# Sparse attention and a squared-ReLU layer on one core: squaring in place, eight mask products on GpSimd, new priorities

## The chip, the cores and the metric

The kernel runs on one core of a Trainium2 chip. The core has a matrix engine (TensorE, PE in the profile), VectorE (DVE), ScalarE (ACT), GpSimd (POOL) and SyncE (SP), and 16 DMA engines that all queues share. POOL and SP issue all the DMAs here. The metric is device time in microseconds of a whole execution; lower is better.

## The reference

Eight batches of eight heads, 576 positions, head size 64. Heads 0 to 3 see a band of 32 positions, heads 4 to 7 every 32nd position. The result, as 4608 tokens of 512, goes through a layer with a squared ReLU.

```python
mask_local = (rel >= 0) & (rel < 32)                    # heads 0..3
mask_strided = (rel >= 0) & (pos[None] % 32 == pos[:, None] % 32)   # heads 4..7
scores = np.where(mask, q @ k.T / 8, -1e9)
attn = softmax(scores)
x = (attn @ v).transpose(0, 2, 1, 3).reshape(4608, 512)
h = x @ w_in                                            # 512 -> 2048
r = np.maximum(h, 0.0)
out = (s * (r * r) + b) @ w_out                         # 2048 -> 512
```

## The kernel before

**Attention.** Each batch is four pairs of heads: m = 0 and 1 are band pairs ("loc"), 2 and 3 strided pairs ("str"). For a pair PE makes the scores of only those blocks that the mask can reach (`score`, L656, into a bank `ps_s`), ACT takes their exponential into `p_loc` or `p_str` (L674), and from batch 1 on one product per pair with a 0/1 mask clears what the mask forbids (`ms`, L682, on DVE, in place). Then PE multiplies by V (`av`, L717, into the banks `ps_a` and `ps_t`), whose rows carry a column of ones, so that the sums of the softmax come with them; DVE inverts those (L734) and scales (L744) into `x_nat`. There are two `p_loc` and two `p_str` tiles, and one bank each of `ps_a` and `ps_t` in the late batches, so that each group of six value products waits for the scaling of an earlier one. `x_nat` is transposed into `xT`, on PE or, later, by DMAs of the SP queue.

**The layer.** Tokens go in nine blocks T of 512. `ff1` (L1016) makes h for 128 features at a time, `rl` (L1042, L1044) the ReLU into a tile `u` of a pool `up` with three buffers of two features each, `sq` (L1050, L1052) the square of such a pair into `gT`, which has two buffers of 16 features. `ff2` (L1271) multiplies by `w_out`. From T = 2 on, `ff2_seven` (L984) does with seven products of half size what takes eight: DVE forms sums of pieces of `gT` (L852) and adds up the products (L903, L915, L926). For T = 7 and 8 `ff1_seven` (L1241) does the same in the first matmul, with ReLU by `add` (L1161) and `relu` (L1169, L1172) into `u` and the square at L1182 and L1184.

**What sets the order.** No engine chooses at run time: each works through its own queue in the order of the program, and PE is where the streams meet. That order comes from a planner (`Plan`) which runs while the program is written. Each PE step, and each piece of work of the other engines ("post"), has keys that it needs, a cost in ns for each engine that may do it, and keys that it makes. Each time that PE's clock moves, the posts that are ready go to the engine that would end first, by their ready time plus a priority from a table `ORDER`; there are four tables, for four stretches of the planner's clock (`UNTIL`). The planner has one clock for each engine and knows of nothing that one engine does to another's speed. POOL's posts are the loads of the next batches (`fetch_qk`: L1356, L387, L390, L405; `fetch_v`: L415, L420), which need the POOL queue for about 0.75 us each, and a few copies.

Of the kernel before, what the change touches and what calls it, by code (L numbers as in the profile page):

```python
# [10 lines left out]
FP16 = mybir.dt.float16  # L11
# [128 lines left out]
class Step:  # L140
    def __init__(self, fn, ns, needs=(), group=None, keys=(), posts=(), after=None):
# [80 lines left out]
def lay_out(ctx, tc, nc, q, k, v, moe_w_in, moe_w_out, moe_s, moe_b, out, order, q_shape, out_shape,  # L222
# [41 lines left out]
    up = ctx.enter_context(tc.tile_pool(name="up", bufs=3))  # L264
# [216 lines left out]
    PE_MASK = 1  # L481
    ps = {f"{tag}{i}": psum.tile([128, PS], FP32, name=f"ps_{tag}{i}")
# [24 lines left out]
    def pair_steps(b, m):  # L507
# [135 lines left out]
        def score(i, group):  # L643
# [18 lines left out]
            if i % per_s == n - 1:  # L662
                key = ("s", id_, g)
                s.keys = [key]

                ng = nt // per_s + (nt % per_s > 0)

                def ex(eng):
                    if "whole" not in st:
                        st["whole"] = p_bufs[loc][p_taken[loc] % len(p_bufs[loc])]  # L670
                        p_taken[loc] += 1
                    at = g * 2 * per_s * nq
                    st["pw", g] = st["whole"][:, at:]
                    nc.scalar.activation(  # L674
                        out=st["pw", g][0:nk, 0:2 * n * nq],
                        in_=st["s", g][0:nk, 0:2 * n * nq], func=AF.Exp, scale=scale)

                def ms(eng):
                    pt = st["whole"][:, 0:2 * nt * nq].rearrange("k (t c) -> k t c", c=nq)
                    mask = (mask_loc if loc else mask_str)[:, None, :].to_broadcast(  # L680
                        [nk, 2 * nt, nq])
                    nc.vector.tensor_tensor(out=pt[0:nk], in0=pt[0:nk], in1=mask, op=ALU.mult)  # L682

                free = [("a", (b - 1, m), 1 if loc else 2)] if b else []
                s.posts = [([key] + free, {"A": 170 + 0.83 * 2 * n * nq}, ex,
                            [("p" if b < PE_MASK else "e", id_, g), group])]
                if b >= PE_MASK and g == ng - 1:
                    s.posts.append(([("e", id_, x) for x in range(ng)],
                                    {"V": 150 + 0.52 * 2 * nt * nq}, ms,
                                    [("p", id_, x) for x in range(ng)]))  # L690
# [315 lines left out]
    def ff1(T, ft, ct, group, cts=(0, 1, 2, 3), early=False):  # L1006
# [23 lines left out]
        if ct == cts[-1]:  # L1030
# [6 lines left out]
            def rl(eng):  # L1037
                if at % 2 == 0:
                    gts["u", T, pair] = up.tile([128, 2, PS], FP16, tag="u", name="u")
                u = gts["u", T, pair][:, at % 2]  # L1040
                if eng == "A":
                    nc.scalar.activation(out=u, in_=gts["h", T, ft], func=AF.Relu)  # L1042
                else:
                    nc.vector.tensor_relu(out=u, in_=gts["h", T, ft])  # L1044

            def sq(eng):
                u = gts["u", T, pair]
                g = gts[T][:, pair[0]:pair[0] + 2, :]
                if eng == "A":
                    nc.scalar.activation(out=g, in_=u, func=AF.Square)  # L1050
                else:
                    nc.vector.tensor_tensor(out=g, in0=u, in1=u, op=ALU.mult)  # L1052

            first = at // 2 * 2
            free = ([("g", T, ff_order(T)[first - 6])] if first >= 6 else
                    [("g", T - 1, ff_order(T - 1)[first - 6])] if T else [])
            s.posts = [([key] + free, {"A": 600, **({"V": 690} if T == 0 else {})}, rl, [("u", T, ft), group])]
# [62 lines left out]
    def ff1_seven():  # L1120
# [3 lines left out]
        for at, (T, u) in enumerate(units):  # L1124
# [28 lines left out]
            def u_at(row, j, st=st, ft=ft):  # L1153
                if ("u", row) not in st:
                    st["u", row] = (xnp if row else up).tile(
                        [128, 2, PS], FP16, tag="xs" if row else "u", name="u")
                return st["u", row][:, :, 256 * j:256 * j + 256]
# [17 lines left out]
            def square(row, st=st, T=T, ft=ft):  # L1175
                def g(eng):
                    if T not in gts:
                        gts[T] = gp.tile([128, NFT, PS], FP16, tag="gT", name="gT")
                    x = st["u", row]
                    g_ = gts[T][:, ft + 8 * row:ft + 8 * row + 2, :]  # L1180
                    if eng == "A":
                        nc.scalar.activation(out=g_, in_=x, func=AF.Square)  # L1182
                    else:
                        nc.vector.tensor_tensor(out=g_, in0=x, in1=x, op=ALU.mult)  # L1184
# [5 lines left out]
            def was(x, old=old):  # L1190
                return [(x,) + old] if old else []

            far = ff_order(T - 1)[8 + 4 * u:12 + 4 * u] if u < 2 else [
                x + y for x in (ft - 4, ft + 4) for y in (0, 1)]
            free = [("g", T - 1 if u < 2 else T, x) for x in far]
# [12 lines left out]
            def wn(n, ft=ft):  # L1208
# [18 lines left out]
                        ([key("c21"), key("c22"), ("F2", T - 2)], SQR, square(1),  # L1227
# [3 lines left out]
                        ([key("c11"), key("c12"), ("F2", T - 2)], SQR, square(0),  # L1231
# [406 lines left out]
```

## Time and profile before

| | us |
|---|---|
| runs of the kernel | 297.75 median (297.03 to 298.77, 3 runs) |
| profiled execution: span from first to last instruction | 295.5 |
| what lies around the span: median less span | 2.25 |
| PE busy | 289.5 (98%) |
| DVE busy | 236.8 (80%) |
| ACT busy | 194.6 (66%) |
| POOL busy | 92.8 (31%) |

Of the profiled execution the page gives the span alone; the 2.25 us beside it are what the runs have more. Only an engine that sets the end can shorten the time when it gets less to do; work of another engine counts where PE has to wait for it.

### The profile page before, as it was taken

The numbers are of one execution on the slowest core, as the hardware profiler recorded it, in microseconds if no ns is written. First come the engines' busy times: TensorE is split into PE (matmuls) and PEld (weight loads), VectorE is DVE, ScalarE is ACT, GpSimd is POOL, SyncE is SP. The second block draws the span as 40 slices with busy tenths as digits, with TensorE's granted clock in tenths as the row PEclk, the third lists the DMA queues.
The fourth block names the chain that finished last, engine by engine and source line by source line (L and its number), as shares of the span: only waits on it lengthen the run. The fifth ranks groups of instructions, "written<-read, shape, count | busy, mean of one in ns | idle before, by whom it ended". The sixth has DMA issues, their size and how long they took to land.

```text
span 295.5 us, 7106 instructions
## 1 busy us (share of the span) xinstructions
PE 289.5 (98%) x2803; PEld 219.3 (74%) x2803; DVE 236.8 (80%) x498; ACT 194.6 (66%) x334; POOL 92.8 (31%) x140
## 2 busy tenths in 40 slices
PE   7899999999999999999999999999999999999995
PEld 3775655665565567989867785779888999999984
DVE  5765977888976789768986888688899689888874
ACT  3667855897967797947873777478966564576500
POOL 8872623610961396008820195200002000000000
PEclk9999999999999999999999999999999999999999
DMA  8999999999999699979999999998430300210314
GB/s 131 180 206 203 213 184 174 208 189 128 140 160 145 98 91 161 160 138 146 162 149 147 169 168 130 134 137 213 44 104 13 109 35 2 71 38 0 109 39 143
DMA packets 106152, 38.19 MB, mean 129 GB/s; under 512 B 85414, under 2 KB 103974, under 8 KB 106118
## 3 DMA queue, kind: packets, MB, share of 16 engines
q0 software_dynamic: 60848, 18.23, 64.2%
q1 hardware_dynamic: 45270, 19.51, 36.1%
q8 instruction: 22, 0.36, 0.5%
q14 instruction: 12, 0.10, 0.1%
HBM read 36.99 MB, written 10.62 MB: 161 GB/s over the span
## 4 chain that ended last, share of the span: by engine, by line
PE 95%; POOL 3%; DVE 1%; issue 1%; ACT 0%; POOLq 0%
PE ps_f L1016 32%; PE ps_f L984 25%; PE ps_f L1271 8%; PE ps_s L656 5%; PE ps_f L1241 3%; PE ps_a L717 3%; PE ps_t L1241 2%; PE ps_s L984 2%; PE ps_a L1241 2%; PE ps_s L1241 2%; PE ps_t L717 1%; PE ps_t L984 1%; PE ps_s L1271 1%; PE ps_f L717 1%; PE ps_t L535 1%; PE ps_f L535 1%
## 5 line engine op out<-in xcount | busy, mean ns | idle before, releaser
L1016 PE MATMUL ps_f<-xT,w_in_sb 128*128 128x512 f16 (+4 forms) x568 | 115.3, 331 | 0.0
L1042 ACT ACTIVATE u<-ps_f 128x512 f16<-128x512 f32 x107 | 62.8, 595 | 34.5 <-PE ps_f L1016 32.4
L1016 PEld LDWEIGHTS <-w_in_sb 128*128 128x128 f16 x576 | 57.1, 114 | 23.1
L984 PEld LDWEIGHTS <-gT 128*128 128x128 f16 x608 | 58.3, 98 | 8.6
L984 PE MATMUL ps_f<-w_out_sb,gT 128*128 128x256 f16 x376 | 53.4, 273 | 0.0
L1271 PE MATMUL ps_f<-w_out_sb,gT 128*128 128x512 f16 x112 | 31.9, 379 | 0.0
L674 ACT ACTIVATE p_str<-ps_s 72x432 f16<-72x432 f32 (+1 forms) x45 | 21.1, 488 | 10.1 <-PE ps_s L656 9.5
L1052 DVE TENSOR_TENSOR gT<-u 128x1024 f16<-128x1024 f16 x32 | 21.8, 682 | 5.2 <-ACT u L1042 4.8
L1050 ACT ACTIVATE gT<-u 128x1024 f16<-128x1024 f16 x24 | 25.4, 1058 | 0.7
L984 PE MATMUL ps_f<-w_mix,gT 128*128 128x256 f16 x176 | 24.9, 273 | 0.0
L674 ACT ACTIVATE p_loc<-ps_s 128x384 f16<-128x384 f32 x46 | 20.7, 489 | 5.5 <-PE ps_s L656 5.1
L744 DVE TENSOR_TENSOR x_nat<-ps_a,rec 72x384 f16<-72x384 f32 (+2 forms) x45 | 23.5, 523 | 0.7
L852 DVE TENSOR_TENSOR gT<-gT 128x1024 f16<-128x1024 f16 x34 | 22.4, 683 | 0.3 <-ACT gT L1050 0.3
L415 POOL DMA_DIRECT2D v_loc<-in_v_dram x24 | 17.8, 767 | 10.1 <-DMA w_out_sb<-in_moe_w_out_dram 4.2
L984 PEld LDWEIGHTS <-S 128*128 128x128 f16 x176 | 17.1, 98 | 2.7
L717 PEld LDWEIGHTS <-p_str 72*128 72x128 f16 x256 | 13.6, 98 | 5.8 <-ACT p_str L674 0.7
L420 POOL DMA_DIRECT2D v_str<-in_v_dram x16 | 13.0, 817 | 12.8 <-PE ps_f L1016 3.7
L1271 PEld LDWEIGHTS <-gT 128*128 128x128 f16 x128 | 11.4, 98 | 6.9 <-issue 0.2
L1356 POOL COPY gate<-kT 1x1 f16<-1x1 f16 x6 | 2.2, 371 | 45.0 <-DMA kT<-ks 45.0
L984 PE MATMUL ps_f<-w_mix,S 128*128 128x256 f16 x112 | 15.0, 273 | 0.0
L734 DVE RECIPROCAL rec<-ps_a 72x6 f32<-72x6 f32 (+2 forms) x45 | 8.3, 184 | 8.4 <-PE ps_a L717 8.0
L717 PEld LDWEIGHTS <-p_loc 128*128 128x128 f16 x192 | 11.2, 98 | 5.0 <-ACT kTs L437 0.8
(235 smaller groups left out, 543.1 us busy)
## 6 DMA issues: line engine op xcount, KB each, us to landing
out_dram<-o SPq DMA_DIRECT2D x34, 256.0 KB
w_in_sb<-in_moe_w_in_dram POOLq DMA_DIRECT2D x4, 512.0 KB, 9.9
w_out_sb<-in_moe_w_out_dram POOLq DMA_DIRECT2D x4, 512.0 KB, 10.7
qs<-in_q_dram POOLq DMA_DIRECT2D x6, 288.0 KB, 8.1
ks<-in_k_dram POOLq DMA_DIRECT2D x6, 288.0 KB, 9.9
v_loc<-in_v_dram POOLq DMA_DIRECT2D x24, 72.0 KB, 9.8
ql<-in_q_dram POOLq DMA_DIRECT2D x4, 288.0 KB, 9.9
kl<-in_k_dram POOLq DMA_DIRECT2D x16, 72.0 KB, 3.7
```

The source lines that it names most:

```text
L415: nc.gpsimd.dma_start(out=vl[LPAD:128, h, :, 0:D], in_=v_band(b, h))
L674: nc.scalar.activation(out=st["pw", g][0:nk, 0:2 * n * nq], in_=st["s", g][0:nk, 0:2 * n * nq], func=AF.Exp, scale=scale)
L717: nc.tensor.matmul(out=st["pa", g][:, n % 6, :], lhsT=st["pw", gp_][0:nk, i * nq:i * nq + WIDE], rhs=vt[0:nk, 2 * mm + e, j, :])
L744: nc.vector.tensor_tensor(out=x_at(0, cnt), in0=st["pa", g][0:nq, 0:cnt, 0:D], in1=st["rec", g][0:nq, 0:cnt].to_broadcast([nq, cnt, D]), o ...
L852: {"V": nc.vector, "P": nc.gpsimd}[eng].tensor_tensor(out=at(out), in0=at(x), in1=at(y), op=op)
L984: nc.tensor.matmul(out=gts[name, T, t][:, 0] if halves else gts[name, T][:, t], lhsT=lhs(k, t), rhs=rhs(k), start=fresh and k == 0 and (ha ...
L1016: nc.tensor.matmul(out=gts["h", T, ft][:, lo:hi], lhsT=w_in_sb[ft // 4][:, ct].rearrange("p (x l) -> p l x", l=4)[:, ft % 4], rhs=xT[ct][: ...
L1042: nc.scalar.activation(out=u, in_=gts["h", T, ft], func=AF.Relu)
L1050: nc.scalar.activation(out=g, in_=u, func=AF.Square)
L1052: nc.vector.tensor_tensor(out=g, in0=u, in1=u, op=ALU.mult)
L1241: nc.tensor.matmul(out=st[bk][:, 256 * t:256 * t + 256], lhsT=lhs(t, c), rhs=rhs(c), start=fresh and t == c == 0, stop=t == c == 1, skip_g ...
L1271: nc.tensor.matmul(out=gts[id_], lhsT=gts[T][:, ft, ts * 128:(ts + 1) * 128], rhs=w_out_sb[:, ft, cols], start=(ft == 0), stop=(ft == NFT ...
```

## The change

Three things.

1. `u` and its pool go. ReLU writes straight into its place in `gT`, and the square is taken there in place, on ACT or DVE as before, with as many instructions of the same sizes. With `u` gone, the ReLU has no wait for a free buffer of it; for T = 7 and 8 the adds and ReLUs now wait until `ff2` of block T - 2 has read its `gT` (key `("F2", T - 2)`), where only the squares did.
2. The mask products of the two band pairs of batches 4 to 7, eight of them, go from DVE to GpSimd (`POOL_MASK = 4`). The planner has them at 4000 ns.
3. All four priority tables have other numbers.

```diff
 UNTIL = (26000.0, 110000.0, 215000.0)
 ORDER = [
-    {"g": 0.0, "S": -2500.0, "in": 500.0, "w_mix": 2500.0, "wc": 0.0, "ev": 2500.0, "c21": -200.0,
...
+    {"g": 0.0, "S": -400.0, "in": -1500.0, "w_mix": 1000.0, "wc": -400.0, "ev": 2500.0,
...
-    up = ctx.enter_context(tc.tile_pool(name="up", bufs=3))
...
+    POOL_MASK = 4
...
-                    nc.vector.tensor_tensor(out=pt[0:nk], in0=pt[0:nk], in1=mask, op=ALU.mult)
+                    on(eng)(out=pt[0:nk], in0=pt[0:nk], in1=mask, op=ALU.mult)
...
                     s.posts.append(([("e", id_, x) for x in range(ng)],
+                                    {"P": 4000.0} if b >= POOL_MASK and loc else
                                     {"V": 150 + 0.52 * 2 * nt * nq}, ms,
...
-                if at % 2 == 0:
-                    gts["u", T, pair] = up.tile([128, 2, PS], FP16, tag="u", name="u")
-                u = gts["u", T, pair][:, at % 2]
+                u = gts[T][:, ft]
...
-                    nc.scalar.activation(out=g, in_=u, func=AF.Square)
+                    nc.scalar.activation(out=g, in_=g, func=AF.Square)
                 else:
-                    nc.vector.tensor_tensor(out=g, in0=u, in1=u, op=ALU.mult)
+                    nc.vector.tensor_tensor(out=g, in0=g, in1=g, op=ALU.mult)
...
-            s.posts = [([key] + free, {"A": 600, **({"V": 690} if T == 0 else {})}, rl, [("u", T, ft), group])]
+            s.posts = [([key], {"A": 600, **({"V": 690} if T == 0 else {})}, rl, [("u", T, ft), group])]
...
-            far = ff_order(T - 1)[8 + 4 * u:12 + 4 * u] if u < 2 else [
-                x + y for x in (ft - 4, ft + 4) for y in (0, 1)]
-            free = [("g", T - 1 if u < 2 else T, x) for x in far]
+            free = [("F2", T - 2)]
```

PE's queue holds the same 2801 matmuls before and after. The first 456 and the last 252 of them stand in the same order; between, the value products of the band pairs of batches 4 to 7 move back. Ahead of the first one of batch 6 (pair 0) there stand, beside what stood there, 8 matmuls of `ff1` of 512 columns, 42 of `ff2_seven` of 256, 16 scores of 144 and 12 value products of 65.

On POOL's queue, before, these are the loads of batch 7: two small copies that wait for the transposed k of batch 6 (`gate`), then q and k, then V.

```order
L1356 COPY gate<-kT_2571 1x1 x2
L387 DMA ql<-in_q_dram 96x6x64 x4
L387 DMA kl<-in_k_dram 96x6x64 x4
L405 DMA qs<-in_q_dram 72x4x512
L405 DMA ks_120<-in_k_dram 72x4x512
L415 DMA v_loc_102<-in_v_dram 96x6x64 x4
L420 DMA v_str_104<-in_v_dram 72x8x64 x4
```

The same place on POOL's queue after the change, and the queue's end:

```order
L1346 COPY gate<-kT_2536 1x1 x2
L387 DMA ql<-in_q_dram 96x6x64 x4
L387 DMA kl<-in_k_dram 96x6x64 x4
L405 DMA qs<-in_q_dram 72x4x512
L405 DMA ks_117<-in_k_dram 72x4x512
L683 TENSOR_TENSOR p_loc_112<-p_loc_112,masks 128x1152
L683 TENSOR_TENSOR p_loc_113<-p_loc_113,masks 128x1152
L415 DMA v_loc_99<-in_v_dram 96x6x64 x4
L420 DMA v_str_101<-in_v_dram 72x8x64 x4
L683 TENSOR_TENSOR p_loc_112<-p_loc_112,masks 128x1152
L683 TENSOR_TENSOR p_loc_113<-p_loc_113,masks 128x1152
```

The two mask products of batch 6 stand behind the gate and the ten loads of q and k of batch 7, and ahead of that batch's V; the last two are those of batch 7. Batch 5 stands in the same way, both products between k and V of the next batch.

POOL's queue after the change at batch 4, where it has its first mask product:

```order
L405 DMA ks_117<-in_k_dram 72x4x512
L683 ISA
L683 TENSOR_TENSOR p_loc_112<-p_loc_112,masks 128x1152
L415 DMA v_loc_99<-in_v_dram 96x6x64 x4
L420 DMA v_str_101<-in_v_dram 72x8x64 x4
L683 TENSOR_TENSOR p_loc_113<-p_loc_113,masks 128x1152
```

The second product has eight loads of V ahead of it, and the first one an instruction without a tile (`ISA`) that before stood ahead of POOL's only product of two tensors, `Ub`, behind all loads.

On DVE's queue, before, at batch 5 (`p_loc_115` and `p_loc_116` are its band pairs, `p_str_117` its first strided pair, `o` stores of block T = 2):

```order
L915 SCALAR_TENSOR_TENSOR o<-ps_f_163,sb_all,Vb 128x512
L682 TENSOR_TENSOR p_loc_115<-p_loc_115,masks 128x1152
L915 SCALAR_TENSOR_TENSOR o<-ps_f_162,sb_all,Ua 128x512
L437 COPY qD_str_110<-qT_2094 64x8x72 x2
L734 RECIPROCAL rec<-ps_a_159 96x6
L734 RECIPROCAL rec<-ps_t_156 96x6
L682 TENSOR_TENSOR p_loc_116<-p_loc_116,masks 128x1152
L744 TENSOR_TENSOR x_nat<-ps_a_159,rec 96x6x64
L744 TENSOR_TENSOR x_nat<-ps_t_156,rec 96x6x64
L915 SCALAR_TENSOR_TENSOR o<-ps_f_163,sb_all,Ub 128x512
L734 RECIPROCAL rec<-ps_a_159 96x6
L682 TENSOR_TENSOR p_str_117<-p_str_117,masks 72x1152
```

The same place on DVE's queue after the change (`p_str_114` is the first strided pair of batch 5):

```order
L917 SCALAR_TENSOR_TENSOR o<-ps_f_160,sb_all,Vb 128x512
L437 COPY qD_str_106<-qT_2060 64x8x72 x2
L917 SCALAR_TENSOR_TENSOR o<-ps_f_159,sb_all,Ua 128x512
L437 COPY qD_str_107<-qT_2060 64x8x72 x2
L917 SCALAR_TENSOR_TENSOR o<-ps_f_160,sb_all,Ub 128x512
L905 SCALAR_TENSOR_TENSOR Va<-ps_f_159,sb_all,bcs 128x512
L854 TENSOR_TENSOR gT<-gT 128x4x256
L683 TENSOR_TENSOR p_str_114<-p_str_114,masks 72x1152
L854 TENSOR_TENSOR gT<-gT 128x4x256
L736 RECIPROCAL rec<-ps_a_156 72x6
L683 TENSOR_TENSOR p_str_115<-p_str_115,masks 72x1152
```

The band pairs' products are gone from it, their scaling (`x_nat` 96x6x64) stands further back, and a sum of two pieces of `gT` now stands right ahead of the first strided pair's product, for which PE's next value products wait.

More of the change, by code (lines that the diff above doesn't have):

```diff
@@ L1046, in sq @@
             def sq(eng):
-                u = gts["u", T, pair]
                 g = gts[T][:, pair[0]:pair[0] + 2, :]
                 if eng == "A":
-                    nc.scalar.activation(out=g, in_=u, func=AF.Square)
+                    nc.scalar.activation(out=g, in_=g, func=AF.Square)
                 else:
[L1052 to L1056, printed above, removed]
-            s.posts = [([key] + free, {"A": 600, **({"V": 690} if T == 0 else {})}, rl, [("u", T, ft), group])]
+                    nc.vector.tensor_tensor(out=g, in0=g, in1=g, op=ALU.mult)
+            s.posts = [([key], {"A": 600, **({"V": 690} if T == 0 else {})}, rl, [("u", T, ft), group])]
             if at % 2:
@@ L1151, in keep, with u_at @@
                 return g
[L1153 to L1157, printed above, removed]
+            def u_at(row, j, T=T, ft=ft):
+                if T not in gts:
+                    gts[T] = gp.tile([128, NFT, PS], FP16, tag="gT", name="gT")
+                return gts[T][:, ft + 8 * row:ft + 8 * row + 2, 256 * j:256 * j + 256]
             def add(row, j, of, name, st=st, u_at=u_at):
@@ L1173, in relu, with square @@
                         "p (t x) -> p t x", t=2))
-            def square(row, st=st, T=T, ft=ft):
+            def square(row, T=T, ft=ft):
                 def g(eng):
-                    if T not in gts:
-                        gts[T] = gp.tile([128, NFT, PS], FP16, tag="gT", name="gT")
-                    x = st["u", row]
                     g_ = gts[T][:, ft + 8 * row:ft + 8 * row + 2, :]
                     if eng == "A":
-                        nc.scalar.activation(out=g_, in_=x, func=AF.Square)
+                        nc.scalar.activation(out=g_, in_=g_, func=AF.Square)
                     else:
-                        nc.vector.tensor_tensor(out=g_, in0=x, in1=x, op=ALU.mult)
+                        nc.vector.tensor_tensor(out=g_, in0=g_, in1=g_, op=ALU.mult)
                 return g
@@ L1226, in ff1_seven @@
                          [key("c21"), Dd]),
-                        ([key("c21"), key("c22"), ("F2", T - 2)], SQR, square(1),
+                        ([key("c21"), key("c22")], SQR, square(1),
                          [("g", T, ft + 8), ("g", T, ft + 9)])]),
@@ L1230, in ff1_seven @@
                        [([key("p3")] + free, COPY, relu, [key("c12"), A]),
-                        ([key("c11"), key("c12"), ("F2", T - 2)], SQR, square(0),
+                        ([key("c11"), key("c12")], SQR, square(0),
                          [("g", T, ft), ("g", T, ft + 1)])]),
```

77 rows, old and new, of the table ORDER are left out of this document.

## The prediction

> **What bounds the kernel now.** I read the page first, then PE's waits, a table by stage, and the last microseconds.
>
> ```profile
> span 295.5 us, 7106 instructions
> PE 289.5 (98%) x2803; PEld 219.3 (74%) x2803; DVE 236.8 (80%) x498; ACT 194.6 (66%) x334; POOL 92.8 (31%) x140
> PE   7899999999999999999999999999999999999995
> ```
>
> PE is busy in every one of the 40 slices but the first two and the last. PE's own waits, and two stretches of the middle (us, then busy time of PE, PEld, DVE, ACT and POOL, clock, DMA share, GB/s):
>
> ```profile
> PE ps_t L527 <- DMA ql<-in_q_dram: 0.9, 1, 0.9
> PE ps_s L1521 <- PEq L1622: 0.8, 1, 0.8
> PE ps_f L717 <- DVE v_loc L437: 0.7, 1, 0.7
> PE ps_f L717 <- POOL v_loc L437: 0.4, 1, 0.4
> ...
> 110.00:160.00 50.00, 50.00 (x495) 40.24 (x494) 40.38 (x86) 35.00 (x59) 19.73 (x30) 1.00 1.36 151
> 160.00:215.00 55.00, 55.00 (x526) 42.66 (x524) 44.91 (x97) 39.45 (x68) 14.22 (x20) 1.00 1.25 143
> ```
>
> All of PE's waits together are 2.8 us, and each of the four belongs to the first batch. From 110 to 215 us, where the change does its work, PE is busy for 105 of 105 us at full clock, while DVE is at 81% of it. So no work taken from DVE, ACT or POOL there can shorten the kernel. What can lengthen it is a result that comes later than PE gets to it. The first 456 matmuls keep their order, so the waits of the start stay; the last 252 keep theirs too, and behind the last matmul stands this tail of 3.1 us:
>
> ```profile
> 291.32 1.04 PE L984 MATMUL ps_f<-w_out_sb,S 128*128 128x256 f16 x8
> ...
> 292.40 0.48 DVE L915 SCALAR_TENSOR_TENSOR o<-ps_f,sb_all,Ub 128x256 f32<-128x256 f32 x1 [0.39 <-PE ps_f L984]
> ```
>
> A gain has no place to come from. The question is what new waits PE gets.
>
> **The change, part by part.** First the squares in place and the products that leave DVE:
>
> ```profile
> L1052 DVE TENSOR_TENSOR gT<-u 128x1024 f16<-128x1024 f16 x32 | 21.8, 682 | 5.2 <-ACT u L1042 4.8
> L852 DVE TENSOR_TENSOR gT<-gT 128x1024 f16<-128x1024 f16 x34 | 22.4, 683 | 0.3 <-ACT gT L1050 0.3
> L682 DVE TENSOR_TENSOR p_loc<-p_loc,masks x14: 714/752/759, 37.0 to 204.3; 128x1152 f16<-128x1152 f16 x14
> ```
>
> DVE takes 683 ns to write over its own input (L852) and 682 from `u` to `gT`, so its squares cost what they did. On ACT no row shows a square in place; I take no change, and ACT's idle third covers some tens of ns more or less. The ReLUs lose a wait that PE never felt, and the adds of T = 7 and 8 gain one whose PE order is unchanged; I put both at 0. Eight products leave DVE: 8 x 0.752 = 6.0 us of its time, worth 0 on PE's path.
>
> What such a product costs on POOL no row shows. The nearest is POOL's only product of two tensors, L926, a quarter of whose time lies beside DVE work (timeline of both engines; start and duration in us):
>
> ```profile
> L926 POOL TENSOR_TENSOR Ub<-Ua,bcs x1: 1649/1649/1649, 221.5 to 221.5; 128x512 f32<-128x512 f32 x1
> L852 DVE TENSOR_TENSOR S<-gT x18: 677/683/1140, 94.3 to 282.6; 128x1024 f16<-128x1024 f16 x18
> ...
> 221.38 0.67 DVE L1099 TENSOR_TENSOR ks<-ks,w_in_sb 128x1024 f16<-128x1024 f16 x1
> 221.54 1.65 POOL L926 TENSOR_TENSOR Ub<-Ua,bcs 128x512 f32<-128x512 f32 x1 [33.35 <-DVE Ua L903]
> 222.60 1.14 DVE L852 TENSOR_TENSOR S<-gT 128x1024 f16<-128x1024 f16 x1 [0.55 <-PE ps_f L984]
> ```
>
> Two things stand here. The DVE sum that starts at 222.60, inside the POOL product (221.54 to 223.19), takes 1.14 us where the median is 0.683: it looks held until POOL is done. And POOL, which starts while DVE is in L1099 (to 222.05), may itself have been held until then, so that 512 elements took 223.19 - 222.05 = 1.14 us. By that rate 1152 elements take 2.6 us, by the whole 1649 ns 3.7 us. I take 2.9: the lower rate and 0.3 for a DVE operation that is under way when POOL comes (half of 0.68). [...]
>
> [...] None of DVE's stores or scalings, which read one tensor from PSUM, ran beside L926; I take them to go on. Now each batch. PE positions come from the row of before, plus or minus the matmuls that the new order puts ahead, at these prices: 0.109 us for 256 columns (16 in 1.75), 0.216 for 512 (8 in 1.73), 0.063 for a score of 144 (3 in 0.19), 0.032 for a value product (6 in 0.19).
>
> ```profile
> 94.06 1.73 PE ps_f L1016 x8
> 263.54 1.75 PE ps_s L984 x16
> 59.80 0.35 PE L656 MATMUL ps_s<-qD_str,kTs 128*72 128x144 f16 x3
> 59.99 0.38 PE L1016 MATMUL ps_f<-xT,w_in_sb 128*128 128x512 f16 x1
> 170.88 0.35 PE L717 MATMUL ps_a<-v_loc,p_loc 128*128 128x65 f16 x6
> 171.07 0.32 PE L717 MATMUL ps_t<-v_loc,p_loc 128*128 128x65 f16 x5
> ```
>
> Batch 6. Its first value products stood at 170.88; 8 x 0.216 + 42 x 0.109 + 16 x 0.063 + 12 x 0.032 = 7.7 us more stand ahead: PE comes at 178.6. The product for them stands in POOL's queue behind the k load of batch 7, which ends at 176.8:
>
> ```profile
> 176.09 0.77 POOL L405 DMA_DIRECT2D ks<-in_k_dram  x1
> ...
> 141.46 0.79 POOL L405 DMA_DIRECT2D ks<-in_k_dram  x1
> 146.97 0.35 PE L717 MATMUL ps_a<-v_str,p_str 72*128 72x65 f16 x6
> 145.07 0.71 DVE L682 TENSOR_TENSOR p_str<-p_str,masks 72x1152 f16<-72x1152 f16 x1
> ```
>
> 176.8 + 2.9 = 179.7: PE waits 1.1 us. The second product ends 2.9 later, 3.5 us of matmuls further on: in time. V of batch 7 is issued some 6 us later than now, ten or more ahead of its use: 0.
>
> Batch 5. The k load ends at 142.2, so POOL is in its two products from 142.2 to 148.0. In DVE's queue a sum of `gT` and the first strided mask product stand there; both wait until 148.0, then take 0.68 + 0.71: 149.4. PE's value products for them stood at 146.97 and now have 10 x 0.109 more and 0.216 + 24 x 0.032 less ahead, so 147.1: PE waits 2.3 us.
>
> Batch 7. POOL has no load left ahead; DVE's product on the first pair began at 200.91 and the scores stand 0.3 us later, so POOL works from 201.2 to 207.0. Two sums and the strided product wait in DVE: 207.0 + 2 x 0.68 + 0.71 = 209.1. PE's value products stood at 209.97 and 2.8 us less stand ahead (ten pairs of 128 and 384 columns, each pair at the price of 512, two of 256, twelve value products): 207.2. PE waits 1.9 us.
>
> ```profile
> 200.91 0.76 DVE L682 TENSOR_TENSOR p_loc<-p_loc,masks 128x1152 f16<-128x1152 f16 x1 [0.22 <-ACT p_loc L674]
> 209.97 0.35 PE L717 MATMUL ps_a<-v_str,p_str 72*128 72x65 f16 x6
> ...
> 108.70 0.75 POOL L405 DMA_DIRECT2D ks<-in_k_dram  x1
> 109.41 3.03 POOL L415 DMA_DIRECT2D v_loc<-in_v_dram  x4
> 112.43 2.43 POOL L420 DMA_DIRECT2D v_str<-in_v_dram  x3
> 113.12 1.21 DVE L878 TENSOR_TENSOR w_out_sb<-w_out_sb 128x2048 f16<-128x2048 f16 x1
> 115.65 0.41 DVE L882 TENSOR_TENSOR bcs<-bcs 128x256 f32<-128x256 f32 x1
> ...
> 113.28 0.35 PE L717 MATMUL ps_a<-v_loc,p_loc 128*128 128x65 f16 x6
> 118.11 0.35 PE L717 MATMUL ps_a<-v_str,p_str 72*128 72x65 f16 x6
> ```
>
> Batch 4. POOL's first product runs from 109.4 to 112.3 and holds back a square, the sum of `bcs`, a `w_mix` difference and the strided product in DVE, 3.0 us together (0.69, 0.4, 1.2, 0.71): 115.3. PE stood there at 118.11 and has 2.6 us less ahead (nine pairs of 192 and 320 columns, two scores and 24 value products less, two of 256 more): 115.5. In time, barely. But SP's queue has one store more ahead of the transposes that open POOL's gate, and its product ends later; if the gate opens 2 us later, PE waits 1.8. I take the middle, 0.9. The second product stands behind eight loads of V (3.03 + 2.43 + 0.8 = 6.3 us): 112.3 + 6.3 + 2.9 = 121.5, and PE comes at 113.28 + 10.1 = 123.4 (32 such pairs, 8 scores, 15 of 256, 32 value products). In time by 1.9.
>
> The sum: 0.9 + 2.3 + 1.1 + 1.9 = 6.2 us. The profiled span would go from 295.5 to 301.7; the median of the runs, 2.25 us above the span, from 297.75 to 304.0. With 2.6 us for a product and the gate as now the four are 0, 1.7, 0.8 and 1.3: 301.6. With 3.7 and the gate 2 us later they are 2.6, 3.9, 1.9 and 3.5: 309.7.
>
> **The rivals.** First, DVE is not held: the 1.14 us was something else. Only one row of eighteen shows it, and L1099, under way when POOL began, took its usual 0.67. Against it: that one row is the only sum beside a POOL product. Then only batch 6's queue costs, 1.1 us: 298.9.
>
> Second, all is hidden, and the time is not above the present one. It turns on POOL's rate: in batch 6 there are 178.6 - 176.8 = 1.8 us, in batch 5 (147.1 - 1.4 - 142.2) / 2 = 1.75, in batch 7 1.95. A product of under 1.75 us costs nothing anywhere. POOL's copies run at such a rate:
>
> ```profile
> L437 POOL COPY v_str<-vs 72x512 f16<-72x512 f16 x4 | 2.3, 611 | 2.1 <-DMA vs<-in_v_dram 2.1
> L926 POOLq MODIFY_POOL_CONFIG  x2: 42/42/42, 188.2 to 188.2; - x2
> ```
>
> 611 ns for 512 is 1.4 us for 1152, but with one input; the row with two needs 2.6. The same end comes if PE reaches these places later than I place it, or the gates open earlier. The time would be 297.8, and since only the start could give anything back, hardly less.
>
> Third, POOL stands still at the instruction ahead of its first product. Before, it was done at 188.2 and the product came 33 us later, so a pause there could not be seen; now nothing lies between. Batch 4 then pays: its second product has 1.9 us of room, and each us beyond that is one of PE. With a pause of 5 us that is 3.1 us in place of 0.9: 306.2. [...]
>
> **How the numbers follow.** Forecast 304.0 with chance 0.58, its own range 301.6 to 309.7. Not held: 0.15, 298.9. All hidden: 0.13, 297.8. The pause: 0.11, 306 to 308. What is left, 0.03, is a gain, which no row offers. Half a per cent, 1.5 us, is about what a measurement of this kernel can tell from no change, so slower means above 299.2: 0.58 + 0.11 and 0.04 of the case not held, 0.73; the same is 0.13 and the other 0.11 of it, 0.24; faster 0.03. From 298.0 to 309.8 about 8 in 10 lie.
>
> **What would show it.** PE waits on POOL `p_loc` in batch 6 and on DVE `p_str` in batches 5 and 7, 1 to 2.5 us each, and PE's slices below 9 there. POOL's rows of L683 between 2.6 and 3.7 us. DVE rows of L854, L1051 and L683 of 2 us and more beside them, and nowhere else. If DVE's rows stay at 0.7 us beside POOL's products, the main term is wrong; if POOL's rows are under 1.8 us, all of it is; if a gap stands between the k load and POOL's first product, it is the third rival.

## The result, and the profile after

The changed kernel takes 320.71 us (median of 4 runs, 316.07 to 323.36), the kernel before 297.61 beside it; the ratio is 1.068 (95% interval 1.061 to 1.074). The forecast was 304.0 with 298.0 to 309.8: the sign was right, the size far too small. Ratios here leave out executions that count as slow (over 1.5% above the fastest of the same kernel), 321.81 and 323.36 among these four, so they are not the quotients of the medians. The profiled execution is the longest of the four, 323.36 us with a span of 321.6. The spans of the others are 314.3, 317.8 and 320.0; the mean granted clock goes from 0.984 in the two shortest to 0.973 in the longest, which is a part of the scatter and not all of it.

The page of the kernel after (span; PE's busy tenths and granted clock in 40 slices):

```profile
span 321.6 us, 7087 instructions
...
PE   8899999999999977997799938999699999999995
...
PEclk9999999999999989999799995999799999999999
```

PE has holes now, four groups of them, and in one slice of each group the clock is low as well. PE's waits (us in total, how many, the longest) and the stretches of the prediction, with one more (us, then busy time of PE, PEld, DVE, ACT, POOL; granted clock, DMA share, GB/s; in the last stretch PE was busy for 35.00 us at clock 1.00 before):

```profile
PE ps_a L719 <- DVE p_str L683: 8.2, 2, 6.0
PE ps_s L657 <- DVE qD_str L437: 6.2, 2, 3.6
PE ps_t L719 <- DMA v_str<-in_v_dram: 1.7, 1, 1.7
...
110.00:160.00 50.00, 42.53 (x397) 34.55 (x395) 43.38 (x66) 28.14 (x50) 31.75 (x38) 0.93 1.51 131
160.00:215.00 55.00, 48.57 (x392) 33.27 (x391) 41.02 (x75) 30.34 (x50) 19.37 (x23) 0.94 1.09 128
215.00:250.00 35.00, 31.76 (x324) 26.74 (x322) 31.03 (x62) 23.26 (x37) 7.11 (x3) 0.95 0.33 74
```

The first three waits are five places, one or two in each of batches 4 to 7: 16.1 us. The clock of 0.93, 0.94 and 0.95 costs, by an estimate, 0.07 x 50 + 0.06 x 55 + 0.05 x 35 = 8.5 us more. Together 24.6 of the 26.1 us by which this span grew. In the shortest execution the clock of 0.984 leaves 0.016 x 314.3 = 5.0 us for that term.

What DVE and GpSimd did there (timeline, start and duration in us; L683 is the mask product, L1051 a square, L854 a sum of `gT`, L437 a copy of Q into `qD_str`, x2 two rows in one):

```profile
111.58 4.11 DVE L1051 TENSOR_TENSOR gT<-gT 128x1024 f16<-128x1024 f16 x1
111.93 0.72 POOL L405 DMA_DIRECT2D ks<-in_k_dram  x1
112.75 2.39 POOL L683 TENSOR_TENSOR p_loc<-p_loc,masks 128x1152 f16<-128x1152 f16 x1
...
123.61 2.37 POOL L683 TENSOR_TENSOR p_loc<-p_loc,masks 128x1152 f16<-128x1152 f16 x1
123.68 2.87 DVE L1051 TENSOR_TENSOR gT<-gT 128x1024 f16<-128x1024 f16 x1
126.47 0.54 DVE L746 TENSOR_TENSOR x_nat<-ps_t,rec 96x384 f16<-96x384 f32 x1
127.06 0.34 PE L719 MATMUL ps_t<-v_str,p_str 72*128 72x65 f16 x6 [1.66 <-DMA v_str<-in_v_dram]
...
147.71 6.84 DVE L437 COPY qD_str<-qT 64x576 f16<-64x576 f16 x1
149.65 4.72 POOL L683 TENSOR_TENSOR p_loc<-p_loc,masks 128x1152 f16<-128x1152 f16 x2
...
186.07 7.09 DVE L854 TENSOR_TENSOR gT<-gT 128x1024 f16<-128x1024 f16 x1
187.88 4.71 POOL L683 TENSOR_TENSOR p_loc<-p_loc,masks 128x1152 f16<-128x1152 f16 x2
...
222.06 4.87 POOL L683 TENSOR_TENSOR p_loc<-p_loc,masks 128x1152 f16<-128x1152 f16 x2 [23.36 <-ACT p_loc L675]
222.24 4.86 DVE L437 COPY qD_str<-qT 64x576 f16<-64x576 f16 x2
```

Read the ends first. The held copy ends at 147.71 + 6.84 = 154.55, 0.2 us after GpSimd's second product (154.37); the held sum at 193.16, 0.6 after (192.59); the square at 115.69, 0.6 after (115.14). So each DVE row lasts until GpSimd is done, and then takes its own 0.2 to 0.6 us. Now the starts. In batches 5 and 6 one DVE row spans both products, and in batches 4 to 6 it begins 1.2 to 1.9 us before the product's row, while GpSimd still shows loads. In batch 7, with no loads right ahead, two copies share 4.86 us: DVE came in between the two products there. The wait at 127.06 is put down to a load of V, but those value products need bank `ps_t`, whose scaling (L746) stood behind the square held until 126.55 and ended at 127.01.

What is open: whether the products alone do this or the new order, what the low clock comes from, and why the hold begins early.

### The profile page after: what moved, and what is told of

It reads as the page before. It is cut to its first block, busy times and chain, and to the rows that moved or that the text cites. A ratio compares the mean times of both kernels' runs of the same rounds, so it can differ in the third digit from the quotient of the medians.

```text
span 321.6 us, 7087 instructions
## 1 busy us (share of the span) xinstructions
PE 298.6 (93%) x2803; PEld 223.0 (69%) x2803; DVE 255.6 (79%) x496; ACT 191.4 (60%) x330; POOL 112.0 (35%) x146
## 4 chain that ended last, share of the span: by engine, by line
PE 78%; DVE 8%; POOL 6%; DMA 4%; issue 3%; SPq 1%; POOLq 0%
PE ps_f L1018 26%; PE ps_f L986 20%; PE ps_f L1261 7%; PE ps_s L657 3%; DVE qD_str L437 3%; DMA v_str<-in_v_dram 3%; PE ps_f L1231 3%; DVE gT L854 3%; PE ps_a L719 2%; PE ps_t L1231 2%; PE ps_s L1231 2%; PE ps_s L986 2%; PE ps_a L1231 2%; PE ps_t L719 1%; PE ps_t L986 1%
## 5 line engine op out<-in xcount | busy, mean ns | idle before, releaser
L1018 PE MATMUL ps_f<-xT,w_in_sb 128*128 128x512 f16 (+4 forms) x568 | 121.6, 341 | 0.0
L1042 ACT ACTIVATE gT<-ps_f 128x512 f16<-128x512 f32 x107 | 63.1, 595 | 44.2 <-PE ps_f L1018 43.4
L986 PE MATMUL ps_f<-w_out_sb,gT 128*128 128x256 f16 x376 | 54.9, 276 | 1.1 <-DVE Va L905 1.1
L1051 DVE TENSOR_TENSOR gT<-gT 128x1024 f16<-128x1024 f16 x32 | 27.5, 860 | 7.6 <-ACT gT L1042 7.1
L1261 PE MATMUL ps_f<-w_out_sb,gT 128*128 128x512 f16 x112 | 29.7, 379 | 0.0
L854 DVE TENSOR_TENSOR gT<-gT 128x1024 f16<-128x1024 f16 x34 | 28.8, 869 | 0.3 <-ACT gT L1049 0.3
L683 POOL TENSOR_TENSOR p_loc<-p_loc,masks 128x1152 f16<-128x1152 f16 x8 | 19.1, 2409 | 23.5 <-ACT p_loc L675 23.4
L1049 ACT ACTIVATE gT<-gT 128x1024 f16<-128x1024 f16 x24 | 25.4, 1057 | 0.7
L746 DVE TENSOR_TENSOR x_nat<-ps_a,rec 96x384 f16<-96x384 f32 (+2 forms) x46 | 24.1, 525 | 0.9
L736 DVE RECIPROCAL rec<-ps_a 96x6 f32<-96x6 f32 (+2 forms) x46 | 8.5, 185 | 15.6 <-PE ps_a L719 15.4
L719 PE MATMUL ps_a<-v_str,p_str 72*128 72x65 f16 x146 | 9.6, 198 | 8.2 <-DVE p_str L683 8.2
```

What stands on the lines that cost most here:

```text
L683: on(eng)(out=pt[0:nk], in0=pt[0:nk], in1=mask, op=ALU.mult)
L719: nc.tensor.matmul(out=st["pa", g][:, n % 6, :], lhsT=st["pw", gp_][0:nk, i * nq:i * nq + WIDE], rhs=vt[0:nk, 2 * mm + e, j, :])
L746: nc.vector.tensor_tensor(out=x_at(0, cnt), in0=st["pa", g][0:nq, 0:cnt, 0:D], in1=st["rec", g][0:nq, 0:cnt].to_broadcast([nq, cnt, D]), o ...
L854: {"V": nc.vector, "P": nc.gpsimd}[eng].tensor_tensor(out=at(out), in0=at(x), in1=at(y), op=op)
L986: nc.tensor.matmul(out=gts[name, T, t][:, 0] if halves else gts[name, T][:, t], lhsT=lhs(k, t), rhs=rhs(k), start=fresh and k == 0 and (ha ...
L1018: nc.tensor.matmul(out=gts["h", T, ft][:, lo:hi], lhsT=w_in_sb[ft // 4][:, ct].rearrange("p (x l) -> p l x", l=4)[:, ft % 4], rhs=xT[ct][: ...
```

## The experiments

### Which of the three parts costs

**All products on DVE, planned anew for that** (new tables, squares in place):

```diff
-    POOL_MASK = 4
+    POOL_MASK = 8
```

> Kernel after, with the batch from which GpSimd takes the mask products set to 8, so that DVE does all of them and the order is worked out anew for that; new priority tables and squares in place stay. My theory (GpSimd's products hold DVE, PE starves, its clock drops): no DVE row of L683, L854 or L1051 above 1.3 us, no PE wait of over 1 us, no half-clock slice between 110 and 240 us, time 297 to 299.5, ratio to before 1.00. Rival A (the new tables' order starves PE by itself): 305 or more. Rival B (squares in place cost): 301 or more, with longer rows of L1051 and L1049.

299.95 us, ratio 1.008 (1.0055 to 1.011), a little over the 297 to 299.5 that I expected.

**The order of the kernel after, with the product issued on DVE at the same places:**

```diff
-                    on(eng)(out=pt[0:nk], in0=pt[0:nk], in1=mask, op=ALU.mult)
+                    nc.vector.tensor_tensor(out=pt[0:nk], in0=pt[0:nk], in1=mask, op=ALU.mult)
```

> Kernel after in the very order planned for GpSimd's products, but the eight products are issued on DVE at the same places of the order. Theory: DVE does each in 0.75 us, nothing is held, 298 to 300, ratio within 0.5 % of before. Rival A (the order itself, a late product behind the DMA issues, starves PE): over 305, with the PE waits of batches 4 to 7 still there. If it lies between, the order carries that part of the loss.

301.66 us, ratio 1.012 (1.007 to 1.016). The stretch where the waits were largest, of these two kernels in turn:

```profile
160.00:215.00 55.00, 54.20 (x509) 41.83 (x508) 45.44 (x97) 35.14 (x64) 14.12 (x20) 1.00 1.32 148
160.00:215.00 55.00, 53.83 (x513) 41.59 (x512) 45.23 (x95) 38.37 (x65) 14.26 (x20) 1.00 1.17 146
```

PE is idle there for 0.8 and 1.2 us, where it was for none before and is for 6.4 in the kernel after. So the new order costs something, about 1%, a little more than I expected of it; it is not where the 7% went.

**The kernel before with the products alone** (old tables, buffers `u` kept):

```diff
+    POOL_MASK = 4
...
-                    nc.vector.tensor_tensor(out=pt[0:nk], in0=pt[0:nk], in1=mask, op=ALU.mult)
+                    on(eng)(out=pt[0:nk], in0=pt[0:nk], in1=mask, op=ALU.mult)
...
+                                    {"P": 4000.0} if b >= POOL_MASK and loc else
```

> Kernel before (old tables, buffers between ReLU and square kept) with only the mask products of band pairs of batches 4 to 7 on GpSimd, planned at the same cost. Theory: the loss comes with the products alone: DVE rows of 2 us and more beside each product, PE gaps of 2 us and more, half-clock stretches of 3.4 us behind them, 308 to 325 us. Rival A (only together with the new tables): under 300. Rival C (the clock drop has nothing to do with the gaps): PE gaps without half-clock stretches, 304 to 312.

319.35 us, ratio 1.073 (1.067 to 1.079): the whole loss, without the other two parts. PE's slices, and in batch 5 what GpSimd and DVE did:

```profile
PE   7899999999999959999699948999799999999995
...
149.01 4.78 POOL L683 TENSOR_TENSOR p_loc<-p_loc,masks 128x1152 f16<-128x1152 f16 x2
151.62 0.75 DVE L917 SCALAR_TENSOR_TENSOR o<-ps_f,sb_all,Ub 128x512 f32<-128x512 f32 x1
152.28 2.13 DVE L683 TENSOR_TENSOR p_str<-p_str,masks 72x1152 f16<-72x1152 f16 x1
```

The same four groups of holes are there. The last two rows begin inside the products (149.01 to 153.79): the store L917, which reads PE's product from PSUM, takes its usual 0.75 us; the strided mask product behind it is held.

**The kernel before with the squares in place alone** (its own tables, products on DVE):

```diff
-                u = gts["u", T, pair][:, at % 2]
+                u = gts[T][:, ft]
...
-                    nc.scalar.activation(out=g, in_=u, func=AF.Square)
+                    nc.scalar.activation(out=g, in_=g, func=AF.Square)
```

> Kernel before with its own tables, squares in place, no products on GpSimd. Theory: same as before within 0.5 % (296.5 to 299), rows of L1051 and L854 at 0.68 us, L1049 at 1.06. Rival B (in place costs through longer rows or through the buffer it has to wait for): over 299.5.

297.40 us, ratio 1.001 (0.999 to 1.003). Squares on DVE and on ACT:

```profile
L1050 DVE TENSOR_TENSOR gT<-gT 128x1024 f16<-128x1024 f16 x32 | 21.8, 682 | 5.2 <-ACT gT L1041 4.8
...
L1048 ACT ACTIVATE gT<-gT 128x1024 f16<-128x1024 f16 x24 | 25.4, 1057 | 0.7
```

### Where the clock goes

**The kernel after with matmuls that nobody reads ahead of the five places where PE waits**, 65 of them, 14 us at 0.216 us:

```diff
+    FILL = {("a", (4, 2)): 9, ("a", (4, 3)): 6, ("s", (5, 3)): 15, ("a", (6, 2)): 24, ("s", (7, 2)): 11}
+
+    def fill(at, group):
+        for _ in range(FILL.get(at, 0)):
+            nc.tensor.matmul(out=bank(group), lhsT=w_in_sb[0][:, 0, 0:128],
+                             rhs=w_in_sb[0][:, 1, 0:512], start=True, stop=True)
```

> Kernel after with idle matmuls (128 x 512, nobody reads them) put ahead of the five places where PE waits: 9 and 6 ahead of the strided value products of batch 4, 15 ahead of the strided scores of batch 5, 24 ahead of the value products of batch 6, 11 ahead of the scores of batch 7; 14 us at 0.216 us each, in gaps of 2.2, 1.7, 3.6, 6.0 and 2.6 us. Theory H (the granted clock halves because PE has stood still): no half-clock slice between 110 and 240 us, DVE's held rows as long as before, time 8 to 9 us shorter than the kernel after: 309 to 314. Rival (the clock falls for another reason, such as power, or falls with GpSimd's products): half-clock slices stay, 319 or more.

315.81 us, ratio 1.058 (1.050 to 1.067): over the 309 to 314 that I expected, and under the rival's 319. The clock's slices are full, and DVE is still held (L865 is the sum of `gT` in this kernel's lines):

```profile
PEclk9999999999999999999999999999999999999999
...
183.42 6.11 DVE L865 TENSOR_TENSOR gT<-gT 128x1024 f16<-128x1024 f16 x1
```

With 14 us more work on PE the clock is back: its mean over the four executions is 0.989 to 1.000, in the kernel after 0.973 to 0.984. So the low clock follows from PE's standing still, and not from GpSimd's products, which are all there. What that is worth in time is less sure. The profiled span of 314.2 is 7.4 us under that of the kernel after, but the latter is the longest of its four; all spans lie from 313.0 to 320.3 with the fillers and from 314.3 to 321.6 without, and the intervals of the two ratios, 1.058 and 1.068, overlap. In the kernel after, windows of 3.41 us around the two waits of batch 4 and the long one of batch 6 show when:

```profile
114.79:118.20 3.41, 1.18 (x18) 0.87 (x17) 3.41 (x5) 0.84 (x2) 3.41 (x6) 1.00 1.30 142
118.20:121.61 3.41, 3.41 (x28) 2.61 (x25) 2.16 (x6) 2.31 (x4) 2.26 (x3) 0.50 1.58 104
...
125.03:128.44 3.41, 1.75 (x26) 1.44 (x24) 3.31 (x8) 1.79 (x3) 1.07 (x3) 1.00 4.02 74
128.44:131.85 3.41, 3.41 (x45) 3.07 (x43) 3.05 (x9) 2.74 (x4) 0.00 (x0) 1.00 1.26 125
...
193.30:196.71 3.41, 2.23 (x16) 1.24 (x17) 3.02 (x7) 0.00 (x0) 3.41 (x6) 0.50 1.18 76
196.71:200.13 3.42, 3.42 (x20) 1.66 (x19) 0.74 (x2) 1.92 (x3) 1.99 (x3) 0.50 1.56 89
```

A window in which PE was busy for 1.18 us is followed by one at half clock, one with 1.75 us is not; and from half clock a window with 2.23 us did not bring it back. The clock stood at 0.50 from 118.20 to 121.61, 155.75 to 159.16, 193.30 to 200.13 and 227.42 to 230.83 us, so the four stretches begin 11, 11 and 10 times 3.41 us apart. In the 3.41 us ahead of them PE was busy for 1.18, 1.06, 0.00 and 0.77 us: it need not stand idle throughout, and one window in which it was busy for a third was enough.

### Why the hold begins early and lasts

**GpSimd's queue drained ahead of each product:**

```diff
+                    if eng == "P":
+                        nc.gpsimd.drain()
                     on(eng)(out=pt[0:nk], in0=pt[0:nk], in1=mask, op=ALU.mult)
```

> Kernel after with GpSimd's queue drained ahead of each of its eight products, so that no product can begin while loads issued ahead of it, or the other product, are still at work. Theory D (in batches 4 to 6 the product holds DVE from before its own row, because it is begun beside the load issues, and two products in a row leave DVE no way in): held DVE rows shrink from 6.8 and 7.1 us to 2.4 to 3, at most one product each, they begin no earlier than the product's row, PE's gaps of 3.6 and 6.0 us fall under 3; time 306 to 314. Rival (the hold is a matter of the two products alone and the row's start is right): rows of 4.7 to 5 us stay, time 316 to 322.

330.34 us, ratio 1.106 (1.094 to 1.117): the time and PE's waits that I expected were wrong, DVE's rows were right. All eight drains (least, median and most, in ns), then DVE and GpSimd in batch 5:

```profile
L684 POOLq DRAIN  x8: 2456/9082/11641, 110.2 to 234.9; - x8
...
156.60 0.61 DVE L437 COPY qD_str<-qT 64x576 f16<-64x576 f16 x2
...
162.15 2.37 POOL L685 TENSOR_TENSOR p_loc<-p_loc,masks 128x1152 f16<-128x1152 f16 x1 [7.08 <-ACT p_str L675]
162.53 2.53 DVE L856 TENSOR_TENSOR gT<-gT 128x1024 f16<-128x1024 f16 x1
164.75 2.53 POOL L685 TENSOR_TENSOR p_loc<-p_loc,masks 128x1152 f16<-128x1152 f16 x1 [0.23 <-ACT gT L1044]
164.99 2.91 DVE L685 TENSOR_TENSOR p_str<-p_str,masks 72x1152 f16<-72x1152 f16 x1
```

No DVE row in it is held before a product's row or past one product. What I had not reckoned with is the drain itself. Three of the eight stand for a product alone; the five behind loads ended 0.4 to 0.8 us after the last of the loads had landed, 5.2 to 9.0 us after that load's row. In batch 5 the row of the last load, that of k, ends at 155.06, the load lands at 161.54, and the drain ends at 161.99. The products came late and PE waited for them, up to 7.1 us. While that drain stood, DVE's copies took their usual time (0.61 us for two of `qD_str`, 5.5 us ahead of the product).

That does not make GpSimd busy until its loads land. In the kernel after, the first product ended at 115.14, and the k load issued ahead of it landed at 122.20. Nor does it show what the issuing of loads does to DVE, since these copies stand behind the rows of the loads. The kernels without a mask product on GpSimd show that: in the kernel before, in the one with squares in place alone and in the two with all products on DVE, no sum, square or mask product of DVE takes longer beside a load than elsewhere (in the kernel before 0.69, 0.69 and 0.76 us at most, the sum of 1.14 beside L926 aside), and a copy at most 0.3 us longer. In the kernel before, beside the k load of batch 6:

```profile
141.50 0.88 DVE L437 COPY qD_str<-qT 64x576 f16<-64x576 f16 x2
```

So the early holds of 1.2 to 1.9 us are not the loads' own doing; it takes a GpSimd operation on the tile behind the loads.

**In place of the product a copy of the tile onto itself** (one input, masks of those pairs left out), and **a fill with ones** (no input; it overwrites what the scores of those pairs gave). The edit of the copy; the fill has `nc.gpsimd.memset(pt[0:nk], 1.0)` in its place:

```diff
+                    if eng == "P":
+                        nc.gpsimd.tensor_copy(out=pt[0:nk], in_=pt[0:nk])
+                        return
```

> Kernel after with GpSimd's eight mask products replaced by copies of the tile onto itself (one input, same tile and size; the masks of those pairs are left out). If any GpSimd operation that reads SBUF holds DVE: DVE rows as long as the copies, 1.4 us each (more for two in a row), PE gaps of 0.5 to 3 us, 302 to 312. If it takes two inputs on GpSimd to hold DVE: DVE rows stay under 1 us, 300 to 302 (as with the products on DVE in the same order).

> Kernel after with GpSimd's eight mask products replaced by a fill of the tile with ones (no input; the masks and the scores of those pairs are left out). If only GpSimd's reads hold DVE: no held rows beside the fills, 299 to 302. If writing is enough: DVE rows as long as the fills, over 302.

301.28 us with the copies, ratio 1.010 (1.0025 to 1.018), and 302.24 with the fills, 1.014 (1.006 to 1.022). Neither can be told from the order with the products on DVE (1.012), so the times decide nothing here. The rows say more; in each fence DVE's and GpSimd's, of the copies first, then of the fills (L857 is the sum, L1054 a square):

```profile
109.38 1.52 DVE L437 COPY qD_str<-qT 64x576 f16<-64x576 f16 x2
110.94 0.69 DVE L857 TENSOR_TENSOR S<-gT 128x1024 f16<-128x1024 f16 x1
...
111.85 1.16 POOL L684 COPY p_loc<-p_loc 128x1152 f16<-128x1152 f16 x1
112.21 1.36 DVE L1054 TENSOR_TENSOR gT<-gT 128x1024 f16<-128x1024 f16 x1
```

```profile
142.68 1.57 DVE L437 COPY qD_str<-qT 64x576 f16<-64x576 f16 x1
...
145.31 2.11 POOL L684 MEMSET p_loc<- 128x1152 f16 x2
146.34 0.68 DVE L857 TENSOR_TENSOR gT<-gT 128x1024 f16<-128x1024 f16 x1
...
203.73 1.06 POOL L684 MEMSET p_loc<- 128x1152 f16 x1 [15.84 <-ACT p_loc L675]
203.94 1.01 DVE L437 COPY qD_str<-qT 64x576 f16<-64x576 f16 x1
```

A GpSimd copy with one input holds a DVE square too (1.36 us, until 113.57; the copy ends at 113.01), but it takes 1.2 us where the product takes 2.4, and PE's longest wait was 1.4 us: the hold came as expected, the 302 to 312 us did not. A fill holds no DVE sum (0.68 us inside it), yet it holds DVE's copies (1.01 us, usual 0.3), which was neither of the two cases that I had written down.

The copy of the tile shows the early beginning best: one GpSimd operation gives two holds, one that ends at 110.90, before its row (1.52 us for two DVE copies, 0.9 more than usual, where loads alone add 0.3 at most), then a sum that runs free (110.94, 0.69 us), and one in the row itself. What GpSimd does with an operation ahead of its row no row shows, so why a hold can begin there is open. Why one DVE row can lie through two products (6.84 and 7.09 us in the kernel after) is open in the same way: that was seen only with loads right ahead, and not in batch 7 nor behind drains.

### How many, and where

**Only the first product of each batch on GpSimd**, and **only the two of batch 7:**

```diff
-                                    {"P": 4000.0} if b >= POOL_MASK and loc else
+                                    {"P": 4000.0} if b >= POOL_MASK and m == 0 else
```

```diff
-    POOL_MASK = 4
+    POOL_MASK = 7
```

> Kernel after with only the first of each batch's two mask products on GpSimd (four in all), the second on DVE, the order worked out anew. [...] Rival (only two products in a row reach PE, a single one is covered by what PE has in hand): 299 to 302.

> Kernel after with the two mask products of batch 7 alone on GpSimd, those of batches 4 to 6 on DVE, the order worked out anew. No loads stand ahead of them. Theory: two holds of one product each, 2.4 us, none that begins ahead of the product's row; one PE gap of 2 to 3 us and 1.7 us of clock, on top of 299.95 us with all products on DVE: 302 to 306. Rival (the hold begins early and spans both products here too): a held row of over 4.7 us, 306 to 309.

One of two: 312.01 us, ratio 1.048 (1.042 to 1.054), 1 us above the 304 to 311 that I expected from holds of 3.5 to 4.5 us in batches 4 to 6, by the 2.4 us of a product and the early 1.2 to 1.9 of the kernel after. Batch 7 alone: 303.11 us, 1.019 (1.016 to 1.022), as expected. The waits and DVE's rows of the first, then of the second:

```profile
PE ps_a L719 <- DVE p_loc L683: 7.6, 3, 2.6
...
111.38 4.10 DVE L1051 TENSOR_TENSOR gT<-gT 128x1024 f16<-128x1024 f16 x1
```

```profile
199.56 2.36 POOL L683 TENSOR_TENSOR p_loc<-p_loc,masks 128x1152 f16<-128x1152 f16 x1 [11.06 <-ACT p_loc L675]
199.88 2.59 DVE L854 TENSOR_TENSOR gT<-gT 128x1024 f16<-128x1024 f16 x1
```

In the first, with loads ahead, a single product makes a DVE row of 3.4 to 4.1 us; in the second, without loads right ahead, one of 2.6 at most. Three waits of 2.5 us (7.6) and three half-clock windows, by an estimate 1.7 us of lost clock each (half of 3.41; the mean clock of 0.983 leaves 0.017 x 310.2 = 5.3), make 12.7 us on the 299.95 with none on GpSimd: 312.6, against 312.01 measured.

## Why the prediction was wrong

The steps from the kernel before to the kernel after, in spans (each kernel differs from the one above by the part named; the second stands by itself):

| kernel | profiled span, us | spans of all executions | step of the profiled |
|---|---|---|---|
| before | 295.5 | 295.3 to 299.4 | |
| before, squares in place alone | 295.6 | 295.3 to 297.3 | +0.1, squares |
| order of after, products on DVE | 297.7 | 297.7 to 300.2 | +2.2, all but GpSimd |
| products on GpSimd, PE kept busy | 314.2 | 313.0 to 320.3 | +16.5, waits |
| after | 321.6 | 314.3 to 321.6 | +7.4, clock |

The third profile is the shortest execution of its kernel and the last the longest, so the +2.2 is the least that the order costs and the +7.4 the most that the fillers show for the clock. The +16.5 is far beyond the scatter.

- **PE bounds the kernel and has nothing to give back**: right. 6 us less work for DVE bought nothing.
- **Squares in place cost nothing**: right, 682 and 1057 ns, before 682 and 1058, ratio 1.001.
- **What a product takes**: 2.40 us, against 2.9 taken and 2.6 by the lower rate. Mis-sized, and on the harmless side.
- **DVE's squares, sums and strided mask products wait while GpSimd is in a product**: the 0.9, 2.3 and 1.9 us of batches 4, 5 and 7 rest on it, and before the change one row alone showed it, of a sum (1.14 us); for squares and strided products it was my estimate. Right in kind: a square took 4.11 and 2.87 us and a sum 7.09, where 0.68 is usual, and with the products alone on GpSimd a strided mask product took 2.13, where 0.71 to 0.75 is usual. Two steps beside it were wrong, and both made the hold too short. I let DVE's copies into `qD_str` go on; they are held as well, and PE waited for them in batches 5 and 7 (6.2 us in all). And I began each hold with the product's row; in batches 4 to 6 it began 1.2 to 1.9 us before, and in batches 5 and 6 a single row then lay through both products, 6.84 and 7.09 us, where I had 5.8.
- **Batch 4: 0.9, the second product in time by 1.9**: 2.2 and 1.7 us. The second product was in time; the square that it held stood ahead of the scaling that empties `ps_t`. I had listed what DVE is kept from for the first product and not for the second.
- **Batch 5: 2.3 at the value products**: 3.6, at the scores, behind the held copy. **Batch 7: 1.9**: 2.6, in the same way.
- **Batch 6: 1.1, PE waits for GpSimd's product behind the k load**: the wrong queue. No PE wait on GpSimd's `p_loc` exists; PE waited 6.0 us for DVE's strided product, which stood behind the sum held for 7.09.
- **The sum of 6.2 us**: 16.1 at those places in the profiled execution. The step that failed is the hold, as above: how long it lasts and which of DVE's operations it reaches.
- **No term for the clock**: the largest omission, 8.5 us by the granted clock in the profiled execution and 5.0 in the shortest; the fillers show 7.4 at most. A wait of PE was priced at its own length; behind four of the five the clock also stood at 0.50 for 3.4 us or, in batch 6, for 6.8.
- **New priorities at nothing**: +2.2 us or more in the span, 0.8% to 1.2% in the ratios. PE waits of up to 1.2 us show in 160 to 215 us; the profiled execution of that kernel is its shortest, so where the rest goes is open.

The rivals fell too. DVE is held, so "not held" is out; "all hidden" needed 1.75 us a product. The pause at GpSimd's configuring instruction did not come: no trace shows the 5 us or more behind the 306 to 308, and in the kernel after the product's row starts at 112.75, 0.1 us after the load ahead of it.

No version of these beats the kernel before; the squares in place alone equal it.

## What to carry to other kernels

Before moving work from DVE to GpSimd, list what DVE does beside it: here its sums (7.09 us for 0.68), squares (4.11 for 0.68), strided mask products (2.13 for 0.71) and copies within SBUF (6.84 for 0.3) waited until GpSimd's product was done, with all that was queued behind them, so the price is the held queue and not the freed time. With loads that GpSimd issued just ahead of such work the hold began up to 1.9 us before the product's row. On a kernel that PE bounds, price a wait of PE at its length and add lost clock: behind the waits of 2.2 to 6.0 us here it was, by an estimate, 1.7 to 3.4 us (half of 3.41 and of 6.83), behind the one of 1.7 us none. And look at the granted clock before explaining a loss by waits alone.

## What the runs showed of the hardware

- Matmuls that nobody reads, put into PE's waits, brought the granted clock back, to 0.989 and more where it was 0.984 and less: 14 us more work on PE, and a kernel that took no longer for it (ratio 1.058 against 1.068).
- A drain of GpSimd's queue behind loads ended only 0.4 to 0.8 us after the last of them had landed, 5.2 to 9.0 us after that load's 0.75 us row; without a drain a product began 0.1 us after such a row.
- DVE holds GpSimd too. In the kernel with the products alone, GpSimd's sum L928 took 3.86 us beside an unbroken row of DVE operations, against 1.65 for the same one before:

```profile
240.86 3.86 POOL L928 TENSOR_TENSOR Ub<-Ua,bcs 128x512 f32<-128x512 f32 x1 [15.71 <-DVE Ua L905]
...
242.31 1.28 DVE L1101 TENSOR_TENSOR v_str<-w_in_sb,ks 128x1024 f16<-128x1024 f16 x2
```

DVE's last such operation ends at 243.59, GpSimd's sum 1.13 us later: the 1.14 us that the prediction read as its true duration.
